# Eight weight places in a new order of opening, and dummy products with split masks in the last attention steps of an attention and spectral-mixing kernel

## The chip, the cores and the metric

The kernel runs on one core of one Trainium2 chip. The metric is the device time of one execution in microseconds. Single runs of one kernel still differ by about 1 us, and now and then by 3 to 6 us, so every experiment was run in five rounds beside the kernel before, on the same chip.

A ratio below is the mean time of one kernel's fast runs over the mean time of the other's of the same rounds, with a 95% interval. It is therefore not quite the ratio of the medians that are quoted.

## The reference, cut to what matters

```python
def reference(q, k, v, w_r, w_i, w_ch):           # names shortened
    # q, k, v: (8, 8, 576, 64); attention over a causal window of 64
    scores = np.matmul(q, k.transpose(0, 1, 3, 2)) / 8
    mask = (rel >= 0) & (rel < 64)
    attn = softmax(np.where(mask, scores, -1e9))
    x = np.matmul(attn, v)                        # -> (8, 576, 512)
    # 64 frequency modes, each with its own complex 512 x 512 matrix
    X = np.fft.rfft(x, axis=1)[:, :64]
    Y = einsum("bmd,mde->bme", X, w_r + 1j * w_i)
    u = x + np.fft.irfft(Y, n=576, axis=1)
    return u + np.maximum(u @ w_ch, 0.0)
```

The mode matrices are two times 64 MB in fp32. They are read once, as 127 loads that land as 512 KB of bf16 each. These loads are the bulk of the work.

## The kernel before

The kernel has three stages: attention (to about 149 us), the 64 modes (to about 392 us), and a tail with the inverse transform and the outputs. Weight loads start during the attention and are all issued by GpSimd, in one order. A load can be issued when its place in SBUF (the memory on the chip) is free. Early places are separate buffers. Later ones are memory that the attention gives back: `kT`, `vT` and so on, and eight "mid" places.

The attention runs in steps `w`. A step makes the scores of block `w` and weighs the values with the block before. The parts that the change touches, with cuts marked:

```python
    def mask(w, times):                  # writes the mask into the score banks; times > 1 only repeats it
        for _ in range(times):
            for hh in range(2):
                ...                      # two or four products of 512 columns

        for w in range(NWIN + 1):
            todo = [...]                 # DFTs, their transposes, the next batch's transposes
            n = len(todo)
            if w < NWIN:
                scores(w)
            if w:
                cut = closes(w - 1)
                weigh(w - 1, 8 * w - 8, cut)       # first part; VectorE then normalizes it
            if todo:
                todo.pop(0)()
            if w + 1 < NWIN:
                mask(w + 1, max(1, 3 - n))         # three times where nothing else is to do
            if todo:
                todo.pop(0)()
            if w:
                weigh(w - 1, cut, 8 * w)           # second part: waits for VectorE
            while todo:
                todo.pop(0)()
            ...                                    # spare(kT), spare(vT): loads into freed memory
        for b in turns:
            dft_turn(b)
        for b in dfts:                             # the last batch
            dft(b)
            dft_turn(b)
    ...
    for j in range(MW):                            # MW = 8 mid places; at: the mode after which a place opens
        at = mode_of(LW + 6 + j) if LW + 6 + j < EARLY else vt_mode
        opens.setdefault(at, []).append(("wm", j, M0 + 2 * (j // 2)))

    def refill_w(m):                               # after mode m: loads into all that is open
        ...
            elif kind == "wm":
                load_w(nw, wmid, f"wm{j}")         # the buffer is made here, in the order of the loads
```

The softmax here doesn't subtract the row's maximum and nothing guards it: scores larger than these inputs give would overflow.

## Time and profile before

| what | value |
|---|---|
| time, median of 3 runs | 430.43 us (430.21 to 431.14) |
| profiled span, mean granted clock (a run of its own, 431.61 us) | 429.8 us, 0.791 |
| last weight wait of TensorE ends (timeline) | 392.45 us |
| from there to the end | 37.35 us |

First, three rows of the page of the kernel before. Each character is one of 40 equal slices (10.7 us): tenths of the granted TensorE clock and of the DMA share, then GB/s.

```profile
PEclk9999999999995555555598988879556665589997
DMA  7999999999999999999999999999999999993898
GB/s 140 213 215 211 213 213 211 213 213 213 214 213 213 198 210 231 212 213 214 213 213 213 213 213 213 214 213 214 213 213 213 213 214 213 213 214 73 265 344 292
```

The DMA engines move 213 GB/s in nearly every slice up to the 36th. The 14th slice has 198. The granted clock (PEclk) is half from about 131 to 216 us. The next line, from the chain that ended last, says that weight loads are its largest part:

```profile
DMA 42%; PE 36%; issue 10%; DVE 7%; ACT 2%; POOL 2%; DVEq 0%; POOLq 0%; ACTq 0%
```

The two places where the DMA rate falls are seen in windows of 2 us of the same kernel. The columns are the window, its length, busy time and instructions per engine, the granted clock, the DMA share and GB/s.

```profile
core 0: us, PE busy (x) PEld busy (x) DVE busy (x) ACT busy (x) POOL busy (x), PEclk, DMA share, GB/s
...
142.00:144.00 2.00, 1.82 (x27) 1.52 (x26) 1.05 (x2) 0.62 (x2) 0.62 (x2) 0.50 0.88 143
144.00:146.00 2.00, 0.83 (x6) 0.41 (x5) 1.05 (x2) 0.00 (x0) 1.05 (x2) 0.50 1.04 209
146.00:148.00 2.00, 1.77 (x4) 0.25 (x2) 0.00 (x0) 0.19 (x1) 0.00 (x0) 0.50 1.09 219
168.00:170.00 2.00, 1.70 (x60) 1.58 (x55) 0.42 (x1) 0.19 (x1) 1.29 (x3) 0.50 0.86 225
170.00:172.00 2.00, 0.82 (x28) 0.82 (x29) 0.00 (x0) 1.47 (x2) 2.00 (x5) 0.50 0.82 150
```

I call them dip (a), at 141 to 144 us, and dip (b), at 169 to 171 us. The waits of GpSimd tell what they come from. A line says who waited for whom, the total in us, the number of times and the longest wait:

```profile
POOL wt L115 <- PE psy L551: 60.0, 14, 13.8
...
POOL kT L115 <- PE pss L291: 10.5, 1, 10.5
```

The wait of 10.5 us stands before dip (a): GpSimd cannot issue the load into `kT` until the last scores have read `kT`. The issue was at 141.56 us. The wait of 13.8 us stands before dip (b): the first of the eight mid loads waited for mode 14, and the seven others, whose memory was free, stood behind it.

### The profile page before, as it was taken

Reading aid. Unit: us, or ns where it says so; the run is one execution under the profiler, and the core shown is the slowest. Engines: PE = TensorE matmul, PEld = TensorE weight load, DVE = VectorE, ACT = ScalarE, POOL = GpSimd, SP = SyncE. Lnnn points to the kernel's source line nnn. Section 1 sums busy time; section 2 is a strip of 40 time slices with the busy share of each in tenths; the row PEclk is TensorE's granted clock in tenths of the full one; section 3 lists DMA queues with packets and bytes.
Section 4 is the critical chain, followed back from the end, with each engine's and each line's share of the span. In section 5 each row is a group of like instructions: output and inputs, shape, how many; then the busy total and the mean of one; then the engine's idle time right before and its main releaser. Section 6 shows DMA issues by size and latency. Waiting matters only on the chain.

```text
span 429.8 us, 11338 instructions
## 1 busy us (share of the span) xinstructions
PE 316.0 (74%) x5057; PEld 228.0 (53%) x5057; DVE 162.0 (38%) x317; ACT 154.6 (36%) x271; POOL 98.3 (23%) x188
## 2 busy tenths in 40 slices
PE   6999999999989776422678888877266652398892
PEld 5665665666654476311566665655244541364681
DVE  5466766666662200306232322212011110042893
ACT  4585866866763121001122222122011110032891
POOL 7131321231020132221121221211111032101510
PEclk9999999999995555555598988879556665589997
DMA  7999999999999999999999999999999999993898
GB/s 140 213 215 211 213 213 211 213 213 213 214 213 213 198 210 231 212 213 214 213 213 213 213 213 213 214 213 214 213 213 213 213 214 213 213 214 73 265 344 292
DMA packets 31104, 92.18 MB, mean 214 GB/s; under 512 B 3424, under 2 KB 3680, under 8 KB 31056
## 3 DMA queue, kind: packets, MB, share of 16 engines
q0 software_dynamic: 25984, 82.55, 96.6%
q1 hardware_dynamic: 4928, 8.78, 5.6%
q8 instruction: 39, 0.64, 0.5%
q10 hardware_dynamic: 144, 0.13, 0.1%
q14 instruction: 9, 0.07, 0.0%
HBM read 162.53 MB, written 9.44 MB: 400 GB/s over the span
## 4 chain that ended last, share of the span: by engine, by line
DMA 42%; PE 36%; issue 10%; DVE 7%; ACT 2%; POOL 2%; DVEq 0%; POOLq 0%; ACTq 0%
DMA wt<-in_moe_w_r_dram 28%; DMA wt<-in_moe_w_i_dram 13%; PE pso L316 6%; PE pst L218 5%; PE psv L235 3%; PE pso L815 3%; PE psx L338 3%; PE pss L272 2%; DVE x_sb L324 2%; PE pss L372 2%; PE pss L291 2%; PE psz L572 2%; PE psy L551 2%; PE psy L546 2%; DVE vT L59 2%
## 5 line engine op out<-in xcount | busy, mean ns | idle before, releaser
L551 PE MATMUL psy<-XQ,wt 128*128 128x16 bf16 x784 | 48.1, 191 | 46.6 <-DMA wt<-in_moe_w_i_dram 44.0
L546 PE MATMUL psy<-XQ,wt 128*128 128x16 bf16 x832 | 52.1, 191 | 31.5 <-DMA wt<-in_moe_w_r_dram 31.0
L551 PEld LDWEIGHTS <-wt 128*128 128x128 bf16 x784 | 37.5, 104 | 51.8 <-DMA wt<-in_moe_w_i_dram 48.7
L546 PEld LDWEIGHTS <-wt 128*128 128x128 bf16 x832 | 39.7, 105 | 36.7 <-DMA wt<-in_moe_w_r_dram 35.0
L115 POOL DMA_DIRECT2D wt<-in_moe_w_i_dram x51 | 27.4, 537 | 99.7 <-DMA wt<-in_moe_w_i_dram 46.8
L572 PE MATMUL psz<-wch,xT 128*128 128x512 f32 x144 | 47.5, 473 | 0.4 <-DVE xT L569 0.4
L115 POOL DMA_DIRECT2D wt<-in_moe_w_r_dram x55 | 29.6, 539 | 77.7 <-DMA wt<-in_moe_w_r_dram 38.4
L569 DVE CAST xT<-pxt 128x512 fp32r<-128x512 bf16 x36 | 23.5, 687 | 63.0 <-PE pxt L566 63.0
L574 ACT CAST Z<-psz 128x512 fp32r<-128x512 f32 x36 | 21.1, 585 | 69.8 <-PE psz L572 61.9
L297 ACT ACTIVATE et<-pss 128x512 bf16<-128x512 f32 x72 | 39.2, 600 | 14.5 <-PE pss L291 14.5
L316 PE MATMUL pso<-vt,et 128*64 128x65 bf16 (+1 forms) x576 | 34.3, 209 | 4.1 <-DVE x_sb L324 4.0
L572 PEld LDWEIGHTS psz<-wch,xT 128*128 128x128 f32 x144 | 29.9, 222 | 6.3 <-issue 0.7
L316 PEld LDWEIGHTS <-et 128*64 128x64 bf16 (+1 forms) x576 | 23.8, 113 | 17.0 <-issue 8.9
L324 DVE TENSOR_TENSOR x_sb<-pso,rcp 128x640 bf16<-128x640 f32 x32 | 26.3, 822 | 0.9
L59 DVE CAST YT<-psy 128x256 fp32r<-128x256 f32 x6 | 2.5, 423 | 60.2 <-PE psy L551 60.2
L833 DVE TENSOR_TENSOR ot<-pso,x_sb 128x512 f32<-128x512 f32 x35 | 22.5, 687 | 3.3 <-PE pso L815 3.0
L272 PE MATMUL pss<-band,ident_bf 64*64 64x512 bf16 x160 | 21.0, 423 | 1.6 <-ACT et L297 1.6
L58 ACT CAST YT<-psy 128x256 fp32r<-128x256 f32 x6 | 2.2, 373 | 54.8 <-DVE YT L59 54.8
L59 DVE COPY vT<-pst 128x768 bf16<-128x768 bf16 x16 | 15.3, 958 | 13.0 <-PE pst L218 13.0
L820 ACT ACTIVATE pso<-pso 128x512 f32<-128x512 f32 x36 | 19.4, 585 | 1.9 <-PE pso L815 1.8
L686 DVE CAST Yb<-psa 96x512 fp32r<-96x512 f32 x8 | 5.5, 687 | 30.4 <-PE psa L680 30.4
L678 PE MATMUL psw<-wch,YT 128*96 128x512 f32 (+1 forms) x36 | 16.3, 598 | 0.2 <-DVE YT L788 0.2
(169 smaller groups left out, 522.0 us busy)
## 6 DMA issues: line engine op xcount, KB each, us to landing
wt<-in_moe_w_r_dram POOLq DMA_DIRECT2D x55, 512.0 KB, 19.1
wt<-in_moe_w_i_dram POOLq DMA_DIRECT2D x51, 512.0 KB, 19.1
out_dram<-ot SPq DMA_DIRECT2D x31, 256.0 KB, 3.5
rk<-in_k_dram POOLq DMA_DIRECT2D x8, 576.0 KB, 10.1
rq<-in_q_dram POOLq DMA_DIRECT2D x8, 576.0 KB, 13.9
rv<-in_v_dram POOLq DMA_DIRECT2D x8, 576.0 KB, 12.7
wy<-in_moe_w_i_dram POOLq DMA_DIRECT2D x4, 512.0 KB, 16.9
kT<-in_moe_w_r_dram POOLq DMA_DIRECT2D x2, 512.0 KB, 9.1
```

The lines of the kernel that those rows point to most:

```text
L59: return nc.vector.tensor_copy(out=o, in_=i)
L115: nc.gpsimd.dma_start(out=wt, in_=src[m].rearrange("(p c) e -> p c e", c=NC))
L218: nc.tensor.transpose(out=ps[64 * hh:64 * hh + 64, c, :], in_=src[:, hh, (c0 + c) * D:(c0 + c + 1) * D], identity=ident_bf)
L272: nc.tensor.matmul(out=pss[(2 * w + hh) % 3][64 * half:64 * half + 64, :], lhsT=ident_bf[pp, pp], rhs=view(band[pp], 128 * half, [[0, WIN ...
L297: nc.scalar.activation(out=et[:, hh, :], in_=pss[(2 * w + hh) % 3], func=ACT_F.Exp, scale=EX_SCALE)
L316: nc.tensor.matmul(out=pso[po, hh, (i // 2) * VW:(i // 2) * VW + D + 1], lhsT=et[pk, hh, col:col + 64], rhs=vt[pk, 1 - f % 2, 2 * hh + g / ...
L324: nc.vector.tensor_tensor(out=view(x_sb, b * NT * DM + g * D, [[4 * D, 2], [DM, NT], [1, D]]), in0=view(pso, 0, [[512, 2], [VW, NT], [1, D]]),
L546: nc.tensor.matmul(out=psy[:, m % MG, e, :], lhsT=wr[:, c, ee], rhs=XQ[:, c, :, 1:3, m], start=(c == 0), stop=(m == 0 and c == NC - 1))
L551: nc.tensor.matmul(out=psy[:, m % MG, e, :], lhsT=wi[:, c, ee], rhs=XQ[:, c, :, 0:2, m], start=False, stop=(c == NC - 1))
L569: nc.vector.tensor_copy(out=xT, in_=pst)
L572: nc.tensor.matmul(out=psz, lhsT=xT[:, c, :], rhs=wch[:, c, :], start=(c == 0), stop=(c == NC - 1))
L833: nc.vector.tensor_tensor(out=ot, in0=ps, in1=x_sb[:, b, t, :], op=ALU.add)
```

## The change

Its intent: (1) open the eight mid places in the order in which their memory is freed, so that GpSimd does not stand behind the one that is freed last; (2) replace the triple masks of the final steps by split masks and dummy products, also around the last DFT, so that TensorE keeps its full clock to the end of the attention and `kT` comes free earlier.

```diff
+    def fill(n):
+        if n > 0:
+            psd = ps_misc.tile([128, WIN], FP32, name="psd", tag="misc")
+            for _ in range(n):
+                nc.tensor.matmul(out=psd, lhsT=warm[:, 0:128], rhs=warm, start=True, stop=True)
+
-    def mask(w, times):
+    def mask(w, times, pair=range(2)):
         for _ in range(times):
-            for hh in range(2):
+            for hh in pair:
 ...
+        LAST_UNITS = max(sched)
 ...
-            if w + 1 < NWIN:
+            if w > LAST_UNITS:
+                mask(w + 1, w + 1 < NWIN, [0])
+            elif w + 1 < NWIN:
                 mask(w + 1, max(1, 3 - n))
             if todo:
                 todo.pop(0)()
             if w:
                 weigh(w - 1, cut, 8 * w)
             while todo:
                 todo.pop(0)()
+            if w > LAST_UNITS:
+                fill(2 - 2 * n)
+                mask(w + 1, w + 1 < NWIN, [1])
 ...
         for b in dfts:
+            fill(3)
             dft(b)
+            fill(3)
             dft_turn(b)
+        fill(2)
 ...
+    mids = {j: wmid.tile([128, NC, DM], BF16, name="wt", tag=f"wm{j}") for j in range(MW)}
 ...
-        at = mode_of(LW + 6 + j) if LW + 6 + j < EARLY else vt_mode
+        at = mode_of(LW + (j > 1) * (EW + 1 - j)) if j else vt_mode
 ...
-                load_w(nw, wmid, f"wm{j}")
+                load_w(nw, wmid, f"wm{j}", mids.pop(j, None))
```

## The prediction

> **What bounds the kernel now.** The DMA engines. The windows view gives 213 GB/s (busy share 1.06) in nearly every stretch to 388 us; 41% of the chain of waits is weight loads. TensorE is 74% busy, but after 180 us it mostly waits for weights: in the timeline the last weight wait ends at 392.5 us. The 37 us that follow run at granted clock 1.00, untouched by the change. So the time is weight stream plus fixed tail, and only time in which the DMA engines run short can be won.
>
> There are two such dips. Windows of 1 us show (a) 141 to 144 us: 188, 143, 143 GB/s, a loss of 165/213 = 0.8 us; (b) 169 to 171 us: shares 0.82 and 0.61 against 1.06, a loss of 0.65 us. In the waits view GpSimd stood 10.5 us before (a), for the last scores to release kT (issue at 141.56), and 13.9 us before (b), for products of mode 14 (issue at 168.71), then sent eight mid loads in a row. The order view shows why: of the eight only the first waits for TensorE, on memory freed last; the others queue behind it.
>
> **What the change does.**
> 1. Mid places: in the new order view the first mid load waits for no product, the next six for modes 6 to 9, only the last for mode 14. By the timeline mode 3 ends near 152.8 and mode 9 near 161 us. Loads then go out as one of eight outstanding transfers lands; dip (b) closes: minus 0.7 us, all critical.
> 2. Dummy products, split masks: in the final steps the clock falls to 0.50 at 130.8 us and stays there to 180 us. The DFT's five products take 1.29 us before the fall, 2.36 to 2.42 after. The Trainium skill, "TensorE: Matmul & The Clock Gate", Part 1, says idleness gates the clock to half; the trace agrees (busy 3.85 of 5 us just before). The change drops the triple masks (ten in 0.83 us) and puts two 128x512 products in idle steps, eight around the last DFT, each about 0.22 us warm (estimate: half of a DFT product's cold 0.43), largely inside waits for VectorE (0.2 plus 0.82 us) and ScalarE. If the clock holds, 130 to 150 us shrinks by 4 to 5 us: last scores near 137 us, modes from 144.5 instead of 149.6. Only dip (a) is worth time: minus 0.8 us. The rest becomes TensorE waiting for weights.
>
> Other engines' orders are unchanged; late in the stream a few mid loads swap the landing they wait for, which should cost nothing.
>
> **Sum.** 430.4 - 0.7 - 0.8 = 428.9 us, -0.35%. Range 427.7 to 430.1. Faster by over 2%: 1%; within 98%; slower 1%.
>
> **What would show each step.** (1) Mid loads spread from about 153 us on, no 13.9 us wait, no dip near 170 us. (2) Clock near 1.00 to the end of the last DFT, which takes 1.3 us; modes 4 to 5 us earlier; no dip at 141 to 144 us. (3) Last weight wait ends near 391 us; tail still 37 us.
>
> **What would make it wrong.** The clock falls all the same (two products a step too few): dip (a) then closes only in part, about 0.5 us lost. Or the shifted stream meets another clock phase at 374 to 394 us, where TensorE has only 0.4 us of slack before each of the last weights: plus or minus 1 us. Or a new shortage of free places later in the stream.

## More of the kernel before

A few pieces of the chain of waits of the kernel before show one of the last steps (start, length, what it was). L316 is the weighing, L291 the scores, L272 the masks.

```profile
130.23 0.89 PE pss L272 x9
...
131.36 0.76 PE pso L316 x7
132.12 0.51 PE pss L291 x14
```

The masks at 130.23 us are the triple ones: nine pieces in 0.89 us. Two of the three do no needed work, but they stand in front of the second part of the weighing (131.36 us), where TensorE has to wait for VectorE anyway.

## The result, and the profile after

The time after is 432.25 us (median of 6 runs, 430.70 to 433.27). The kernel before gave 430.53 us in its 6 runs. The ratio is 1.0034 [1.0013, 1.0055]: slower by 0.3%. That is within 2%, but outside the predicted range and on the other side of the kernel before. The profiled span is 431.5 us at a mean clock of 0.796. The last weight wait of TensorE ends at 394.15 us instead of 392.45, and the tail is 37.35 us in both. So all of the loss is in the weight stream.

The same three rows of the page, of the kernel after:

```profile
PEclk9999999999995675555588988689556655589997
DMA  8999999999999799999999999999999999993898
GB/s 141 211 213 213 213 213 213 213 212 213 214 213 213 148 210 260 214 214 213 214 213 214 213 213 213 214 213 213 213 213 214 213 213 215 213 213 63 260 351 289
```

The dip in the 14th slice has become deeper (148 instead of 198 GB/s), and from about 129 to 214 us the clock is half for nearly as long (75 us in three stretches, 85 us before). The windows of the kernel after:

```profile
core 0: us, PE busy (x) PEld busy (x) DVE busy (x) ACT busy (x) POOL busy (x), PEclk, DMA share, GB/s
...
142.00:144.00 2.00, 1.25 (x19) 0.83 (x20) 0.69 (x1) 0.38 (x1) 0.00 (x0) 0.66 0.50 100
144.00:146.00 2.00, 1.83 (x35) 1.61 (x31) 0.83 (x2) 1.09 (x2) 1.06 (x2) 0.50 0.39 47
146.00:148.00 2.00, 1.67 (x23) 0.90 (x21) 0.22 (x1) 0.00 (x0) 0.00 (x0) 0.50 0.89 143
168.00:170.00 2.00, 0.88 (x30) 0.80 (x27) 0.00 (x0) 0.00 (x0) 0.53 (x1) 0.50 1.09 288
170.00:172.00 2.00, 0.82 (x29) 0.82 (x29) 0.00 (x0) 0.00 (x0) 0.53 (x1) 0.50 1.27 377
```

Dip (b) is gone: 288 and 377 GB/s at 168 to 172 us, where other transfers run as well, instead of 225 and 150. Dip (a) has grown to 6 us and a low of 47 GB/s. The waits of GpSimd in the kernel after (L568 and L298 are L551 and L291 of before, moved by added lines):

```profile
POOL wt L115 <- PE psy L568: 48.4, 16, 7.5
...
POOL kT L115 <- PE pss L298: 10.7, 1, 10.7
```

No wait is longer than 7.5 us now, and the 13.8 us before dip (b) are gone, as the new order was meant to do. The wait for the last scores is about as long as before, but it ends later: the `kT` load is issued at 144.66 us, 3.10 us later than before. About 1.0 us of that is luck: the whole attention started later, because the first warm-up products took longer (14 passes took 6.00 us, 5.09 us before; the same code). The other 2.08 us lie between the issue into `vT` and the issue into `kT`: 15.50 us before and 17.58 us after. One profile each would not show that this is the change. The experiments below give more: these steps as they were before took 13.37 to 15.50 us in seven profiles (the kernel before, e1, e4, e6, e14, e17, e18; least where the clock was low for only 3.4 us of them), and as the change made them 16.81 to 17.58 us in three (the kernel after, e2, e16). The two ranges do not meet.

The chain of waits of the kernel after shows where. L323, L298 and L279 are the weighing, the scores and the masks; L265 is the dummy products.

```profile
132.98 0.83 DVE x_sb L331
133.86 0.90 PE pso L323 x8
134.76 0.97 PE psd L265 x2
135.73 0.20 PE pss L279
135.92 0.74 PE pss L298 x13
```

Only half a mask was left to issue in front of the wait for VectorE, which ends with its normalization (`x_sb`, from 132.98 us, 0.83 us). Then the second part of the weighing, two dummies (0.97 us), the second half of the mask and the scores follow one after the other. The step's scores start at 135.92 us: dummies and mask stand in front of them, on the path. And the clock had fallen all the same at 129.0 us. In the step before this one TensorE idled 1.99 us (127.47 to 129.46 us) in front of the second part, where the triple masks used to be. All profiles together say that this is the cause: the clock falls 1.3 to 1.9 us after the issue into `vT` where only half a mask stands in this wait (the kernel after, e2, e3, e16), 4.2 to 5.3 us after it where whole masks do, and 11 us or more after it where dummies stand there too (e5, e8, e10 to e13, e15).

### The profile page after: what moved, and what is told of

Same layout as the page of the kernel before. It is cut to its first block, busy times and chain, and to the rows that moved or that the text cites. A ratio compares the mean times of both kernels' runs of the same rounds, so it can differ in the third digit from the quotient of the medians.

```text
span 431.5 us, 11315 instructions
## 1 busy us (share of the span) xinstructions
PE 319.0 (74%) x5038; PEld 229.8 (53%) x5049; DVE 161.9 (38%) x317; ACT 154.8 (36%) x271; POOL 98.5 (23%) x188
## 4 chain that ended last, share of the span: by engine, by line
DMA 46%; PE 32%; issue 11%; DVE 7%; ACT 2%; POOL 1%; DVEq 0%; POOLq 0%; ACTq 0%
DMA wt<-in_moe_w_r_dram 32%; DMA wt<-in_moe_w_i_dram 13%; PE pso L323 6%; PE pst L218 5%; PE psv L235 3%; PE pso L832 3%; PE pss L379 3%; PE psx L345 2%; DVE x_sb L331 2%; PE pss L298 2%; PE pss L279 2%; DVE vT L59 2%; PE psd L265 1%; ACT vt L58 1%; PE psy L563 1%
## 5 line engine op out<-in xcount | busy, mean ns | idle before, releaser
L568 PE MATMUL psy<-XQ,wt 128*128 128x16 bf16 x784 | 48.2, 191 | 46.8 <-DMA wt<-in_moe_w_i_dram 40.9
L568 PEld LDWEIGHTS <-wt 128*128 128x128 bf16 x784 | 37.6, 104 | 52.4 <-DMA wt<-in_moe_w_i_dram 46.0
L589 PE MATMUL psz<-wch,xT 128*128 128x512 f32 x144 | 48.9, 485 | 0.4 <-DVE xT L586 0.4
L323 PE MATMUL pso<-vt,et 128*64 128x65 bf16 (+1 forms) x576 | 34.4, 209 | 6.7 <-DVE x_sb L331 6.6
L323 PEld LDWEIGHTS <-et 128*64 128x64 bf16 (+1 forms) x576 | 23.7, 113 | 19.1 <-issue 11.3
L279 PE MATMUL pss<-band,ident_bf 64*64 64x512 bf16 x136 | 20.2, 408 | 1.3 <-ACT et L304 0.9
L298 PE MATMUL pss<-qT,kT 64*64 64x128 bf16 (+1 forms) x640 | 17.3, 221 | 0.5 <-issue 0.5
```

The lines of the kernel that those rows point to most:

```text
L279: nc.tensor.matmul(out=pss[(2 * w + hh) % 3][64 * half:64 * half + 64, :], lhsT=ident_bf[pp, pp], rhs=view(band[pp], 128 * half, [[0, WIN ...
L298: nc.tensor.matmul(out=pss[(2 * w + hh) % 3][64 * half:64 * half + 64, col:col + nq], lhsT=kTs[b % 2][pp, g, 64 * kb:64 * kb + 64], rhs=qT ...
L323: nc.tensor.matmul(out=pso[po, hh, (i // 2) * VW:(i // 2) * VW + D + 1], lhsT=et[pk, hh, col:col + 64], rhs=vt[pk, 1 - f % 2, 2 * hh + g / ...
L568: nc.tensor.matmul(out=psy[:, m % MG, e, :], lhsT=wi[:, c, ee], rhs=XQ[:, c, :, 0:2, m], start=False, stop=(c == NC - 1))
L589: nc.tensor.matmul(out=psz, lhsT=xT[:, c, :], rhs=wch[:, c, :], start=(c == 0), stop=(c == NC - 1))
```

## The experiments

The letters in the texts name theories in the order in which they came up. Those that matter: A, dummies and half masks that stand in front of the scores lie on the path; C, the end of the stream follows the issue of the last `kT` load one for one; E, the early dip near 170 us depends on how early the modes start; F, G and H, three causes of a dip at 343 to 353 us (the new mid order, a slow TensorE there, too few places); I, J, K, three causes of what the last section finds. "vT to kT" is the interval between the two issues named above. "Last wait" is the end of TensorE's last wait for a weight, and "kT" the issue time, all from the profiled run. The profiled run of the kernel before (431.61 us) was slower than all six of its timed runs, so its last wait may be later than usual.

| run | median us (before, same rounds) | ratio [95%] | vT to kT | kT | last wait |
|---|---|---|---|---|---|
| kernel before | 430.53 | | 15.50 | 141.56 | 392.45 |
| kernel after | 432.25 (430.53) | 1.0034 [1.0013, 1.0055] | 17.58 | 144.66 | 394.15 |
| e1_mids_only | 431.02 (430.73) | 0.9993 [0.9960, 1.0025] | 15.39 | 142.91 | 392.63 |
| e2_fills_only | 435.11 (430.73) | 1.0081 [1.0039, 1.0123] | 17.46 | 143.47 | 396.18 |
| e3_split_no_step_fill | 431.67 (430.73) | 1.0022 [0.9980, 1.0064] | 16.95 | 146.99 | 396.61 |
| e4_triple_masks_back | 431.35 (430.73) | 0.9999 [0.9965, 1.0032] | 15.30 | 143.10 | 392.56 |
| e5_fill_in_wait | 430.70 (431.00) | 0.9986 [0.9955, 1.0016] | 12.06 | 137.65 | 391.85 |
| e6_late_start | 430.72 (431.00) | 0.9999 [0.9961, 1.0036] | 14.79 | 141.42 | 391.31 |
| e7_dft_held | 430.64 (431.00) | 0.9985 [0.9951, 1.0019] | 13.18 | 141.13 | 391.80 |
| e8_dft_held_fill | 430.92 (431.00) | 0.9991 [0.9960, 1.0022] | 11.94 | 137.71 | 391.87 |
| e9_one_mask_in_wait | 430.86 (430.62) | 1.0007 [0.9991, 1.0023] | 14.77 | 142.25 | 391.63 |
| e10_fill_in_wait_old_mids | 431.03 (430.62) | 1.0013 [0.9992, 1.0034] | 12.31 | 138.89 | 391.88 |
| e11_fill_in_wait_late_warm | 430.81 (430.62) | 1.0004 [0.9990, 1.0018] | 12.30 | 137.87 | 392.08 |
| e12_old_mids_late_warm | 430.64 (430.62) | 1.0003 [0.9989, 1.0017] | 12.10 | 138.39 | 391.77 |
| e13_fill_extra_place | 430.54 (430.46) | 1.0022 [0.9993, 1.0051] | 12.07 | 137.66 | 391.29 |
| e14_before_extra_place | 431.00 (430.46) | 1.0012 [0.9997, 1.0027] | 13.43 | 140.26 | 391.40 |
| e15_held_fill_extra_place | 430.59 (430.46) | 0.9998 [0.9984, 1.0013] | 11.95 | 139.80 | 391.63 |
| e16_after_extra_place | 432.86 (430.46) | 1.0051 [1.0011, 1.0090] | 16.81 | 144.48 | 393.92 |
| e17_more_rows | 447.12 (430.89) | 1.0384 [1.0337, 1.0431] | 13.39 | 141.31 | not used |
| e18_more_time | 434.89 (430.89) | 1.0092 [1.0058, 1.0125] | 13.37 | 139.25 | not used |

All outputs are right.

### Which part costs: e1 to e4

**e1_mids_only**: the kernel before with only the mid places changed (the three last pieces of the diff).

> The kernel before with the new order of the mid places alone. Theory A (the mid places are worth what was predicted; the final attention steps cost the rest): the dip near 170 us is gone, the one at 141 to 144 us stays at about 0.8 us, the last weight wait ends 0.7 us earlier, time 0.7 us under the kernel before (about 429.8). Rival B (the mid places themselves cost, by other memory or a later shortage): at or above the kernel before, up to +1.5 us.

No gain: 0.9993. Dip (b) is closed in its profile. So the part that does what it was meant to do is worth nothing that can be seen, where I had put 0.7 us. (Its interval alone does not rule 0.7 us out; those of e11 to e13, which close both early dips, do.)

**e2_fills_only**: the kernel after with the old mid order.

> The changed kernel with the old order of the mid places: dummy products and split masks alone. Theory A: both dips, the first one about 3 us long, kT issued 2 to 3 us later than before, time 2 to 2.5 us over the kernel before. Rival B: time at or under the kernel before.

Slower by 0.8%, with both dips. The dummies and split masks carry the loss, and with them the old mid order hurts too: the late modes make dip (b) longer (3.4 us of full rate). Beside steps that end late the new order is worth something after all: 1.0081 without it, 1.0034 with it, though in different rounds.

**e3_split_no_step_fill**: the kernel after without the dummies in the steps.

```diff
-                fill(2 - 2 * n)
```

> The changed kernel without the two dummy products per step (those around the last DFT stay, masks stay split). Theory A1 (the cost is the dummy products' place: after the second part of the weighing, ahead of the scores, on the path, 0.9 us a step in two steps before the last scores): kT is issued about 2 us earlier than in the changed kernel, time about 1.5 us under the changed kernel. Theory A2 (the cost is the split of the masks, which leaves the wait for VectorE bare, so the clock falls earlier and everything runs cold): no better than the changed kernel, or worse, since even less keeps the clock up.

Inconclusive as a time. The interval is 16.95 us, only 0.63 us less than in the kernel after. In its profiled run the clock had also been low at 67 to 77 us, so its absolute times are late.

**e4_triple_masks_back**: the kernel after with the old triple masks in the steps and no dummies there; the dummies around the last DFT stay.

```diff
-            if w > LAST_UNITS:
-                mask(w + 1, w + 1 < NWIN, [0])
-            elif w + 1 < NWIN:
+            if w + 1 < NWIN:
                 mask(w + 1, max(1, 3 - n))
...
-            if w > LAST_UNITS:
-                fill(2 - 2 * n)
-                mask(w + 1, w + 1 < NWIN, [1])
```

> The changed kernel with the old triple masks and no dummy products in the steps; the eight around the last DFT stay, and the new mid places. Theories A1 and A2 both: the final steps take as long as before (kT issued near 141.6 us, first dip 0.8 us), the second dip stays closed: time 0.7 us under the kernel before, as in the run with the mid places alone; the last DFT may be 0.5 to 1 us faster without effect. If it is 1 us or more above that run, the dummy products around the DFT cost by themselves.

15.30 us, as before the change, and no loss is seen (0.9999, though the interval reaches 1.0032; the trace says it more clearly). So the split masks and step dummies cost the 2 us, and the DFT dummies cost nothing that shows.

### Is it their place: e5, e9

**e5_fill_in_wait**: both masks and the dummies stand inside the wait for VectorE, before the second part of the weighing; none at the DFT. Mid places as in the change.

```diff
             if w > LAST_UNITS:
                 mask(w + 1, w + 1 < NWIN, [0])
+                fill(0 if n else 8 if w == LAST_UNITS + 1 else 4)
+                mask(w + 1, w + 1 < NWIN, [1])
...
-            if w > LAST_UNITS:
-                fill(2 - 2 * n)
-                mask(w + 1, w + 1 < NWIN, [1])
```

> New mid places and split masks, but dummy products (8 in the first final step, 4 in the others without DFT work) and the second mask stand inside the wait for VectorE, before the second part of the weighing, none ahead of the scores or round the last DFT. From vT's issue to the last kT's issue GpSimd took 15.5 us before, 17.6 in the changed kernel, 15.3 to 15.4 where the triple masks stood. Theory A2 (the bare wait for VectorE let the clock fall, and the cold steps cost): the clock stays up longer and the interval is 13 to 15 us. If instead dummy products cost wherever they stand: 16 us or more, and a time over the run with the mid places alone. The second dip stays closed either way.

This is what the change had intended. The interval falls to 12.06 us, `kT` is issued at 137.65 us, four microseconds earlier than before the change. Windows of this kernel:

```profile
142.00:144.00 2.00, 1.61 (x8) 0.52 (x6) 0.30 (x1) 0.27 (x1) 0.61 (x2) 1.00 1.08 217
144.00:146.00 2.00, 0.70 (x15) 0.58 (x16) 0.42 (x1) 0.70 (x2) 0.00 (x0) 1.00 1.06 215
...
168.00:170.00 2.00, 1.06 (x37) 0.95 (x33) 0.00 (x0) 0.00 (x0) 0.53 (x1) 0.50 1.17 303
170.00:172.00 2.00, 0.00 (x0) 0.00 (x0) 0.15 (x3) 0.00 (x0) 0.85 (x3) 0.50 1.07 216
...
349.00:353.00 4.00, 3.07 (x40) 2.28 (x38) 0.69 (x1) 0.58 (x1) 2.43 (x5) 0.50 0.95 163
```

Both early dips are gone. But the time is 0.9986 of before [0.9955, 1.0016]: no gain that can be told from none. And a new dip has come at 349 to 353 us.

**e9_one_mask_in_wait**: as e3, but with both masks of the pair in the wait.

```diff
             if w > LAST_UNITS:
-                mask(w + 1, w + 1 < NWIN, [0])
+                mask(w + 1, w + 1 < NWIN)
...
-            if w > LAST_UNITS:
-                mask(w + 1, w + 1 < NWIN, [1])
```

> The changed kernel without step dummies, and with both masks of a pair together inside the wait for VectorE (one pair, not three): against the run with split masks and no step dummies, only the second mask moves, from in front of the scores into the wait. Theory A3 (the second mask in front of the scores lies on TensorE's path): interval from vT to kT 15.0 to 15.8 us instead of 16.95, though the clock is low all the same. Theory A2 (only the clock counts, and the bare wait lets it fall): interval stays near 17 us.

14.77 us against 16.95 us in e3: the place of one half mask makes up to 2.2 us over five steps. It is not the path alone. The clock fell at about 132 us in both, but that is 1.7 us after the issue into `vT` in e3 and 4.5 us after it in e9, so the mask in the wait also kept the clock up for longer. Theory A is supported; how the 2.2 us divide between the path and the clock is not shown.

### Does the time follow kT: e6, e7, e8

**e6_late_start**: the kernel before with nine instead of seven warm-up products, so that everything starts later.

> The kernel before with 9 warm-up products at the start instead of 7: two more at about 0.53 us each (fp32 128x256, two passes of 0.26 us when warm), 1.06 us more before the first transpose and nothing else. Theory C (in all six profiles the last weight wait ends 249.5 us after the last kT's issue when the second dip is closed, 250.9 before: while the first dip exists the time follows kT's issue one for one, so it is TensorE's attention chain and not the stream alone that sets the time): 0.8 to 1.1 us slower than before, interval from vT to kT unchanged at 15.5. Rival D (the stream is the limit from the first microsecond and TensorE has slack in attention): no change.

The time does not follow: 0.9999. In the profiled run the premise failed, though: the interval was shorter by chance (14.79 us), so `kT` was issued no later than before (141.42 us). And it says nothing of the 1.0 us of bad luck in the profile of the kernel after, where the wait for `kT` leaves no room. e2 has the same steps and started 1.07 us earlier; by the count of "starved" time that is explained in the last section of the experiments, its engines starved for 0.37 us at dip (a), those of the kernel after for 1.24 us. So this luck probably is a part of the loss in that one profile. Its six runs, 430.70 to 433.27 us, also lie further apart than those of the kernel before (430.21 to 431.14 us).

**e7_dft_held** holds the seventh batch's DFT back until the last scores are out, with the new mid places and the old masks; **e8_dft_held_fill** does so on e5.

```diff
-            turns[:] = dfts
-            todo += [lambda b=b: dft(b) for b in dfts]
-            dfts.clear()
+            if not LAST_UNITS < w < NWIN:
+                turns[:] = dfts
+                todo += [lambda b=b: dft(b) for b in dfts]
+                dfts.clear()
```

> New mid places and old triple masks, no dummy products; the DFT of the seventh batch and its turn, 2.4 and 0.6 us of TensorE ahead of the last scores, are held back until after the last scores. Theory C: kT's issue comes 2.5 to 3 us earlier (interval 12.5 to 13 us), the first dip closes, time 1 to 1.5 us under the run with the mid places alone, near 429; it can't gain the whole 3 us, because the stream is then unbroken. Rival D: no gain, the work is only moved.

> The run with the DFT held back, with dummy products inside the waits as in the run before that. Both dips closed with more room: interval 11 to 12.5 us if the clock stays up; time within 0.3 us of the run with the DFT held back alone where that one's stream is unbroken, but less spread from run to run, since a late attention is absorbed.

The interval is 13.18 and 11.94 us, the first hardly below the 13.37 to 15.50 us of the unchanged steps, and neither run is faster beyond its interval. Up to here, `kT` had been moved over 9 us, from 137.65 to 146.99 us. The last wait follows it where it is late, at about 249.5 us behind it in the kernel after and in e16. It does not follow where it is early: 254.2 us behind in e5. Theory C holds on one side only.

### Is it the new dip at 343 to 353 us: e10 to e16

**e10_fill_in_wait_old_mids** is e5 with the old mid order. **e11_fill_in_wait_late_warm** is e5, and **e12_old_mids_late_warm** is e10, with dummy products in the weight waits of the odd modes 49 to 55, which are meant to keep TensorE's clock up there:

```diff
+            elif m < M0 + B:
+                mode(m, lambda: idle(0, 4))
+                idle(0, 2)
             else:
                 mode(m)
```

> Dummies and both masks in the wait for VectorE, old order of the mid places. The attention chain is then short (interval near 12 us). Theory E (the second dip was only a consequence of late modes: mode 14 comes early enough if attention ends early): no dip near 170 us in spite of the old order. Theory F (the new order takes away one late load's lead, the second load of a pair at 338.4 instead of 335.2 us, and so makes the dip at 343 to 352 us): no dip there, 75.2 MB or more moved by 355 us, last weight wait about 390.8, time near 429.5. Rival G (in 320 to 352 us TensorE, cold and doing the spectrum, sets the pace whatever the order): a loss of about 1 us there again, time near 430.5.

> The run with dummies in the wait (new mid places) plus dummy products in the waits for weights of the odd modes from 49 to 55, where the places run short. Rival G (TensorE at half clock sets the pace in 320 to 352 us): clock near 1 there, the loss of 1.2 us at 343 to 352 us goes, last weight wait about 390.7, time about 1 us less. Theory F (the order of places alone): the loss stays.

> Both: old mid places, dummies in the waits of attention and of modes 49 to 55. Under F or G: no dip after 20 us, last weight wait 390.5 to 391, time 429 to 429.5, the best of all; if it is still at 430.3 or more, a further limit stands behind.

In e10 there is no dip near 170 us even with the old order (theory E: early modes alone close it), and the dip at 343 to 353 us is there as well (F falls). The dummies kept the clock up only in part, but enough to judge: in e11 it was 1.00 at 341 to 345 us and the rate was still 182 GB/s, in e12 it was 0.94 at 349 to 353 us and the rate still 168 GB/s (G falls). None of the times moved.

**e13_fill_extra_place**, **e14_before_extra_place**, **e15_held_fill_extra_place** and **e16_after_extra_place** give e5, the kernel before, e8 and the kernel after one more place of 512 KB from mode 48 on:

```diff
+    wx = ExitStack()
+    wxp = wx.enter_context(tc.tile_pool(name="wxtra", bufs=1, reuse_waits="tile"))
+    free.append(("wx", 0, NM))
...
+            if kind == "wx":
+                load_w(nw, wxp, "wx")
+            elif kind == "wl":
```

> Dummies in the wait, new mid places, one more place from mode 48 on. Theory H (the number of open places limits the stream at 343 to 353 us once it comes early): no dip there, about 75.5 MB moved by 355 us instead of 75.1, last weight wait near 390.3 instead of 391.85, time about 1.3 us less than without the place, near 429.3. If the dip stays, neither order, clock nor places is the limit.

> The kernel before with the extra place. Theory H: its stream comes too late to run short there (no dip at 343 us before), so no change, within 0.4 us of the kernel before.

> DFT held back, dummies in the wait, new mid places, extra place. Theory H: as the first of these runs, no dip from 20 us to 388 us, time near 429.2.

> The changed kernel with the extra place. Theory H and C: no help, since the last kT's issue sets the time; last weight wait again 249.5 us after kT's issue, interval from vT to kT 17.5 us again, time within 0.5 us of the changed kernel's (0.2 to 0.5 percent over the kernel before).

In e13 the dip is gone, so its cause was places (H). The weight stream now has no dip left up to 385 us, and still there is no gain (1.0022 [0.9993, 1.0051]). Its last windows tell why. The first is where the dip was, the others are the end of the stream:

```profile
349.00:353.00 4.00, 1.87 (x39) 1.46 (x37) 0.69 (x2) 0.58 (x1) 1.87 (x4) 0.92 1.07 214
385.00:387.00 2.00, 2.00 (x24) 1.03 (x22) 0.00 (x0) 0.00 (x0) 0.00 (x0) 1.00 0.67 133
387.00:389.00 2.00, 1.51 (x9) 0.45 (x9) 0.00 (x0) 0.00 (x0) 0.00 (x0) 1.00 0.51 102
389.00:391.00 2.00, 1.90 (x20) 0.84 (x17) 0.00 (x0) 0.00 (x0) 0.00 (x0) 1.00 0.38 76
```

The rate falls to half at 385 us, and the remaining data take until 391 us at half rate. The kernel before, at its end:

```profile
387.00:389.00 2.00, 1.58 (x20) 0.91 (x20) 0.00 (x0) 0.00 (x0) 0.00 (x0) 1.00 1.06 213
389.00:391.00 2.00, 1.56 (x21) 0.83 (x20) 0.00 (x0) 0.00 (x0) 0.00 (x0) 1.00 0.60 119
391.00:393.00 2.00, 1.53 (x21) 0.71 (x20) 0.00 (x0) 0.00 (x0) 0.00 (x0) 1.00 0.18 35
```

The kernel before keeps the full rate up to 389 us. It stops about 1 us later than e13, with a shorter stretch at half rate. The engines have moved the same data: most of what e13 had gained by closed dips it gave back here. e14 and e15 are no faster either (1.0012 and 0.9998), and e16 shows that the extra place does not help the kernel after (1.0051).

### What is behind the half rate

The trace has sixteen landings for each load. The Trainium skill says why ("DMA: Bandwidth & Descriptors", "Why a DMA increments its semaphore by 16 and not by 1"): for loads like these, all sixteen DMA engines post a completion of their own. I call the time between the first and the last of the sixteen the spread. It is how far the fastest engine runs ahead of the slowest. Counts from the records of the kernel before, around each instruction fetch from 200 us on, for the last load that landed before the fetch and for the first that landed at least 3 us after it started:

```
fetch starts us   engines within 0.5 us of the last   spread us
   203.3                  2 -> 3                     1.91 -> 1.94
   218.5                  3 -> 4                     1.94 -> 1.87
   230.3                  4 -> 5                     1.91 -> 1.89
   243.1                  5 -> 6                     1.87 -> 1.94
   255.3                  6 -> 7                     1.91 -> 1.87
   269.7                  7 -> 8                     1.91 -> 1.93
   282.5                  8 -> 1                     1.88 -> 2.63
   297.3                  1 -> 2                     2.62 -> 3.00
   312.5                  2 -> 3                     3.02 -> 2.98
   332.1                  3 -> 4                     3.01 -> 3.01
   346.9                  4 -> 5                     3.01 -> 3.01
   361.9                  5 -> 6                     3.00 -> 3.01
   383.6                  6 -> 7                     3.01 -> 2.98
```

Each fetch moves exactly one more engine back into the last group. When eight are there, the next fetch starts a new group behind them. The landings do not name their engines, but this staircase has one plain reading: the fetches of instructions are taken by eight engines in turn, and the other eight take none. The fetches are in the page of the kernel before (queue and kind: packets, MB, share):

```profile
q0 software_dynamic: 25984, 82.55, 96.6%
...
q8 instruction: 39, 0.64, 0.5%
```

39 packets of 16 KB. The Trainium skill ("Runtime: NRT & Kernel Launch", "Instruction fetch mechanics") says that instructions come in blocks of 16 KiB for 256 of them, and that the cost of crossing such a boundary is "mostly hidden". The size agrees with this trace: the profile page counts 5,057 products and 5,057 weight loads on TensorE, and 10,114 / 256 is 39.5. The passage is about the engine that runs the instructions. A stream that fills the DMA engines does pay: a fetch takes 0.89 to 1.16 us of one engine, and before 141 us each round of eight fetches adds about 1.1 us to the spread (1.3 us at 70 us, 2.4 at 90, 3.5 at 130).

That gives the reading of the dips, in numbers of the same records:

```
                 spread us at       spread, last weight   weights end us   starved us
                 140   150   175    load
kernel before    3.5   1.8   0.7          3.0                392.10          0.08
e1_mids_only     3.6   0.7   1.7          4.0                392.27          0.02
kernel after     3.6   0.4   1.6          3.8                393.77          1.24
e5_fill_in_wait  3.5   3.7   3.7          2.9                391.50          0.00
e13 (no dips)    3.7   3.7   3.6          5.9                390.93          0.00
```

"Starved" is the time between 20 and 380 us with fewer than eight packets under way, each moment weighted by the share of eight that is missing. A dip first stops the eight engines that are ahead, because they have done their part of all the loads that were issued. The eight that lag still have work. The packets under way show it: of usually 16 or more, at least 8 stay in the whole of dip (a) of the kernel before, while in the kernel after there are fewer than 8 for about 1.9 us. The end of the eight that lag is the end of the stream. Dip (a) of the kernel before cost 0.8 us of sixteen engines, as the prediction said, but that is 1.6 us of eight, and the spread shows whose: it fell by 1.7 us (3.5 to 1.8). With the dip closed (e5, e13), the eight leaders only get further ahead. In e13 they finish 5.9 us before the last one.

In the kernel after the gap was too long for that. From the windows above, 142 to 148 us lost (113 + 166 + 70) x 2 / 213 = 3.3 us of sixteen engines, or 6.6 us of eight. The spread took 3.2 us of it (3.6 to 0.4). What is left is (6.6 - 3.2) / 2 = 1.7 us in which both halves stood; the direct count gives 1.24 us. The end of the weights moved by 393.77 - 392.10 = 1.67 us, and the median time by 1.72 us. The size is right; the agreement to the tenth is chance, since even the runs with next to no starved time differ by 1.3 us. The runs with more than 1 us starved are the kernel after, e2, e3, e16, e17 and e18 (1.24, 2.98, 3.39, 1.11, 14.00 and 3.69 us); all the others have at most 0.10, with the weights ending between 390.93 and 392.27 us.

### A direct try on the fetches: e17, e18

Before I had looked at the landings, I tried to lengthen the lag. **e17_more_rows** adds 34 dummy products of one column to each of 31 modes, for about eight more fetches. **e18_more_time** adds three wide ones instead, as a control for TensorE's time. `extra` was added on both sides of the mode's second wait:

```diff
+    def extra(m, n):
+        if m < 17 or 38 <= m < M0 or m >= M0 + B:
+            psd = ps_a.tile([128, DM], FP32, name="psd", tag="psw")
+            for _ in range(n):                     # e17: 17 and 17, w = 1; e18: 1 and 2, w = 512
+                nc.tensor.matmul(out=psd[:, 0:w], lhsT=ident_bf, rhs=view(x_sb, 0, [[1, w]]),
+                                 start=True, stop=True)
```

> The kernel before plus 34 tiny dummy products (one column each) in each of 31 frequency modes that have waits for weights: 2,100 more TensorE instructions, hardly any more memory traffic. Counts of the packets that I draw from the traces: the weight stream ends with only about eight of the sixteen DMA engines still at work (before: full until 389.4 us, end 392.1), and the 39 instruction fetches of 16 KB take eight durations in turn, as if they used eight engines in turn. Theory I (the fetches load eight engines only, and those eight set the end of the stream): 47 fetches, 8.2 more, so about one more on each of the eight: the last weight lands 0.9 to 1.1 us later (around 392.0 by the trace, where the undisturbed runs gave 390.9 to 391.5), and the stretch with half of the engines gets 0.9 to 1.1 us longer; the time is 0.8 to 1.1 us longer (ratio 1.002). Rival J (the lag has another origin, such as slower engines; fetches do not matter): the last landing stays at 390.9 to 391.5, ratio 1.000 within its interval. Rival K (TensorE's extra work frees places later): end later, but the control run e18 shows the same.

> Control for the run with more rows: the same TensorE time in the same 31 modes, as 3 wide dummy products (512 columns) each in place of 34 tiny ones: only 190 more instructions, so at most one more fetch. Theory I: last landing and time as in the kernel before (390.9 to 391.5 us, ratio 1.000 to 1.001). Rival K (places freed later by TensorE's extra work): as late as the run with more rows, 0.8 us or more.

Neither came as any theory had it. The number of fetches did: 48 and 40 instead of 39. The times did not (1.0384 and 1.0092). Two lines of the windows from 140 us on, first of e17, then of e18:

```profile
160.00:180.00 20.00, 15.30 (x542) 15.11 (x540) 3.27 (x26) 2.54 (x5) 0.66 (x3) 0.50 0.52 124
180.00:200.00 20.00, 15.49 (x510) 14.81 (x508) 9.76 (x33) 3.80 (x10) 6.65 (x13) 0.50 0.82 158
```

```profile
160.00:180.00 20.00, 18.80 (x437) 15.05 (x433) 9.05 (x45) 5.41 (x12) 4.79 (x9) 0.97 0.78 173
180.00:200.00 20.00, 19.39 (x158) 10.40 (x159) 5.65 (x15) 3.11 (x8) 4.23 (x8) 0.60 1.06 214
```

From 160 to 180 us TensorE catches up with early modes whose weights have long landed. There it had no slack, which I had not checked: the tiny products took 165 ns each, so the places came free late and the DMA engines starved (124 GB/s in that window). In e18 the wide products had also kept the clock at 0.97, so it was no control for e17. Both runs confirm only what a real shortage does: the weights end at 407.52 and 395.50 us, later by about the starved time of 14.00 and 3.69 us (without it, 393.5 and 391.8 us). That e17 is 1.7 us beyond e18 is in the direction of theory I, but the run is too disturbed to show it. What additional fetches cost by themselves is not measured by them. It rests on the staircase above.

## Why the prediction was wrong, point by point

- **"The time is weight stream plus fixed tail"**: right. The tail is 37.35 us in both, and the loss of 1.7 us is in the stream.
- **"Only time in which the DMA engines run short can be won"**, and the terms **"minus 0.7 us, all critical"** and **"Only dip (a) is worth time: minus 0.8 us"**: mis-sized. The dips were real, with these areas, but they were idle time of the eight engines that run ahead. e1 closes dip (b) for 0.9993, e5 closes both for 0.9986; their intervals are too wide to rule out the 0.9965 that was predicted. e13 does: it has no dip left up to 385 us, and its ratio is 1.0022 [0.9993, 1.0051].
- **Step 1, mid places**: the mechanism was right. The 13.9 us wait is gone, and so is the dip near 170 us. Only the worth was wrong: nothing that shows in e1, and something only beside late steps (e2).
- **Step 2, "largely inside waits for VectorE ... and ScalarE"**: this is the step that failed and made the kernel slower. The change puts the dummies and the second half mask behind the wait and in front of the next scores, and takes the triple masks out of the wait. Instead of 4 to 5 us less, the interval to the last scores took 2.08 us more. With the triple masks back (e4) it is as before; with dummies and both half masks inside the wait (e5) it is 12.06 us, 3.4 us shorter than before.
- **"If the clock holds"**: it did not; it fell at 129.0 us. The Trainium skill ("TensorE: Matmul & The Clock Gate", Part 1) has an idle window of about 3.4 us put the clock to half, with a window that runs freely. The two values of the granted clock, 0.50 and 1.00, agree, and so does the window: the low stretches here last 3.41 us or a multiple of it. The trigger does not: in the 3.4 us before the fall TensorE was still busy for 1.9 us (2.6 us in the kernel before), so the 1.99 us of idleness where the masks had been were enough. I had named a falling clock as a danger, but priced it as half a gain lost. I had not asked what the removed masks did for the wait.
- **Step 3, "tail still 37 us"**: right.
- **"A new shortage of free places later in the stream"**: did not come in the kernel after. It came in e5 at 343 to 353 us, e13 removed it with one more place, and neither mattered.

Three things stay open. How much of the loss in the one profile of the kernel after comes from its late start, and how much from the steps, is not measured. Among the runs without starved time the weights end anywhere from 390.93 to 392.27 us, and I cannot attribute this 1.3 us. And that fewer TensorE instructions would end the stream earlier, by about 1.1 us for 2,048 of them (an estimate from the spread's growth for eight fetches), follows from the staircase, but no run has tried it. No version that I ran beats the kernel before outside its interval.

## What to carry to other kernels

In a stream like this one, a dip in the total DMA rate is worth time only if the engine that finishes last is idle in it: look at the sixteen landings of a load, and compare the dip with the spread before counting its area as a gain. Filler work for the clock has to stand in front of a wait that exists anyway; behind the wait it is simply more work, and a filler that is removed may have been holding the clock. Before work is added "in the waits" of a stage, check that this stage has waits, stretch by stretch.

## What the Trainium skill lacked or had wrong

- "Runtime: NRT & Kernel Launch", "Instruction fetch mechanics", calls the cost of crossing a 16 KiB boundary mostly hidden and does not give what a fetch costs a DMA stream: here 0.89 to 1.16 us of one engine for each of 39 fetches.
- No page that I read says that the fetches go to eight of the sixteen DMA engines in turn. Here, as read from the landings, each one moved one more engine back, and eight fetches added about 1.1 us to the spread of a load's landings.
- "Perfetto Trace Analysis", "What 'DMA-bound' means", names specific DMA engines as one possible bound and points to a track for each engine. The views used here have no such tracks. The aggregate showed 213 GB/s, and the bound showed in the sixteen landings per load (3.0 us apart at the end, 5.9 us in the run without dips) and in a half rate at the end of the stream.
- "DMA: Bandwidth & Descriptors", "Latency and other measured facts", says that engines 7 and 15 are usually slower. The landings here do not name their engines, so no run tests it; the group that lags grew by one engine per fetch, from 2 to 8 between 203 and 270 us, and is not a fixed pair.
